# Sparse attention with MLP on one core: keys and values kept on row (token mod 128), values cast in place, SyncE and GpSimd in written order

## The chip, the cores and the metric

The kernel runs on one core of one Trainium2 chip. The metric is the device time of one execution in microseconds (us), on that core. Before the change the median of three runs is 268.42 us (268.03 to 269.17).

Engine names in the profile: PE is TensorE (PEld its weight loads), DVE is VectorE, ACT is ScalarE, POOL is GpSimd, SP is SyncE, SPq its DMA-issuing part.

## The reference

Sparse attention over 4 batches, 8 heads, 768 tokens and head size 64, followed by a two-layer MLP on the 3,072 tokens:

```python
k_sum = k.reshape(B, H, nb, 32, D).max(axis=3)      # one maximum key per block of 32
v_sum = v.reshape(B, H, nb, 32, D).mean(axis=3)     # one mean value per block
mask_l = np.abs(pos[:, None] - pos[None, :]) < 16   # local window
scores = concat([where(mask_l, q k^T * scale, -1e9), q k_sum^T * scale + log(32)])
x = softmax(scores) @ concat([v, v_sum])            # [B, H, S, D] -> [B*S, 512]
h = x @ w_in                                        # 512 -> 2048
out = (h * sigmoid(beta * h)) @ w_out               # 2048 -> 512
```

## The kernel before

Work is done in pairs of heads, four pairs to a batch, and in query tiles of 64. A query tile sees 96 window keys and 24 block keys, so 120 rows of a 128-row operand. The kernel builds these operands by copying: `kw` by VectorE from transposed keys, `vw` by 13 DMAs per batch. "(b, g)" below means pair g of batch b. Each batch has an **H stage** (16 h tiles, between them the keys and queries of the next batch) and an **O stage** (24 o parts, between them the attention of the next batch). Batch 0's attention has nothing to hide behind; it is **the head**.

```python
    # ... sizes: B=4, H=8, S=768, D=64; block=32, window=16, QT=64, KW=96, nb=24, VW=129; P=128
    q_r, k_r, v_r = (a.rearrange("b (g h) (c p e) d -> b g p (h c) (e d)", p=P, h=2, e=NE)
                     for a in (q, k, v))
    # ... 12 loads of batch 0 (k, q, v of four pairs) issued from SyncE and ScalarE; the later ones in stage()
    def load_pair(dst, src, b, g, nm):
        t = qk_pool.tile([P, nc3, NE, 2, D], bf16, name=nm, tag=nm)
        nc.gpsimd.tensor_copy(out=t[:], in_=stage(src, b, g, nm))
        dst[(b, g)] = t

    def load_v(b):
        for g in range(npair):
            nc.gpsimd.tensor_copy(
                out=vn_bufs[0][:, :, :, g, 0:2 * D].rearrange("p c e (h d) -> p c e h d", h=2),
                in_=stage(v_r, b, g, "v"))

    # ... constants on GpSimd: identity, bias, A_avg (block means as a matmul), band masks
    def scale_w_out(n):
        nc.vector.tensor_scalar(out=w_out_sb[:, n], in0=w_out_sb[:, n], scalar1=inv_beta[:, n:n + 1],
                                scalar2=None, op0=ALU.mult)
    def v_windows(b):
        vn, vw, vm = vn_bufs[0], vw_bufs[b % 2], vm_bufs[b % 2]
        vm_ps = ps.tile([P, npair, 2 * D], f32, name="vm_ps", tag="t", bufs=2)
        n = nc3 * NE
        for c in range(nc3):
            for e in range(NE):
                i = c * NE + e
                nc.tensor.matmul(vm_ps[:], A_avg[:, c, :], vn[:, c, e, :, 0:2 * D],
                                 start=(i == 0), stop=(i == n - 1))
        nc.vector.tensor_copy(out=vm[KW:P, :, 0:2 * D], in_=vm_ps[KW:P])
        vt = vw.rearrange("p (c u) g d -> p u c g d", u=P // QF)
        U = P // QF
        for e in range(NE):
            r0 = e * KF
            for u in range(U):
                lo, hi = u * QF - WF, u * QF - WF + KF
                a, z = max(lo, 0), min(hi, P)
                nc.sync.dma_start(out=vt[r0 + a - lo:r0 + z - lo, u], in_=vn[a:z, :, e])
                if lo < 0:
                    nc.sync.dma_start(out=vt[r0:r0 - lo, u, 1:], in_=vn[P + lo:P, 0:nc3 - 1, e])
                if hi > P:
                    nc.sync.dma_start(out=vt[r0 + P - lo:r0 + KF, u, 0:nc3 - 1], in_=vn[0:hi - P, 1:, e])
        nc.sync.dma_start(out=vw[KW:P], in_=vm[KW:P, None].to_broadcast([P - KW, nt, npair, VW]))

    def prep_pair(b, g):
        i = (b * npair + g) % NKW
        kw, q2 = kw_bufs[i], q2_bufs[i]
        kt, qt = ks.pop((b, g)), qs.pop((b, g))
        kwv = kw[:, :, 0:KW].rearrange("p t (e f) -> p t e f", e=NE)
        pk = ps.tile([P, NE, NF], bf16, name="pk", tag="t", bufs=2)
        for c in range(nc3):
            for e in range(NE):
                nc.tensor.transpose(pk[:, e, c * P:(c + 1) * P], kt[:, c, e], identity)
        inner = pk[:, :, QF - WF:QF - WF + KF]
        nc.vector.tensor_copy(out=kwv[:, 1:nt - 1],
                              in_=bass.AP(tensor=inner.tensor, offset=inner.offset,
                                          ap=[inner.ap[0], [QF, nt - 2], [NF, NE], [1, KF]]))
        nc.vector.tensor_copy(out=kwv[:, 0, :, WF:KF], in_=pk[:, :, 0:KF - WF])
        nc.vector.tensor_copy(out=kwv[:, nt - 1, :, 0:KF - WF], in_=pk[:, :, NF - KF + WF:NF])
        km = at_pool.tile([P, nb], bf16, name="km", tag="km")
        mid = kwv[:, :, :, WF:WF + QF]
        nc.vector.tensor_reduce(out=km.rearrange("p (t n) -> p t n", t=nt),
                                in_=bass.AP(tensor=mid.tensor, offset=mid.offset,
                                            ap=[mid.ap[0], mid.ap[1], [FB, QF // FB], mid.ap[2], [1, FB]]),
                                op=ALU.max, axis=mybir.AxisListType.XY)
        nc.vector.tensor_copy(out=kw[:, :, KW:KW + nb], in_=km[:, None].to_broadcast([P, nt, nb]))
        # ... the same for q: six transposes into pq, then copies into q2 on ScalarE and VectorE

    # ... scores(): s_ps = kw x q2, Exp on ScalarE into attn, mask on VectorE (batch 0: on TensorE)
    # ... av(): six matmuls a[:, t] x vw[:, t, g], reciprocal and two multiplies on VectorE into x_nat
    # ... x_transpose(): six transposes into px, copy into xT.  h_tile(): 8 matmuls + Silu.  o_part(): 4 matmuls
    for i in range(4):          # w_in, then w_out: issued from GpSimd, the scheduler decides when
        ...
    v_windows(0)
    prep_pair(0, 0)
    prep_pair(0, 1)
    all_scores(0, 0)
    prep_pair(0, 2)
    all_scores(0, 1)
    prep_pair(0, 3)
    all_scores(0, 2)
    load_beta()
    finish(0, 0)
    all_scores(0, 3)
    for g in range(1, npair):
        finish(0, g)
    # ... per batch: h_tile x 16, between them v_windows and the four prep_pair of the next batch;
    #     then (batch 0 only) the 16 scale_w_out; then o_part x 24, between them scores, av, x_transpose
```

A scheduler orders the instructions of every engine; the kernel's text fixes only what depends on what.

The softmax here doesn't subtract the row's maximum and nothing guards it: scores larger than these inputs give would overflow.

## Time and profile before

| | before |
|---|---|
| time, median of 3 | 268.42 us |
| span of the profiled run | 266.6 us |
| TensorE busy | 224.2 us (84%) |
| GpSimd busy | 49.3 us (18%) |
| DMA bytes | 35.83 MB |
| first h matmul of batch 0, which ends the head | 54.93 us |
| from there to the first h matmul of batch 1, then 2, then 3 | 53.27, 54.11, 54.12 us |
| rest (last batch) | 50.2 us |

The last three rows are read from TensorE's timeline: the start of the first `h_ps` matmul of each batch. They add up to the span, so a change of time can be put down to a stage.

The first lines to read are those of the page that cut the span in 40 slices of 6.7 us (busy tenths of TensorE, its granted clock in tenths, DMA busy tenths, and GB/s). Kernel before:

```profile
PE   0006924689999999999999999999999999999984
PEclk9999785979999999999999999999999999999999
DMA  7999999998799966119983111130011121000112
GB/s 194 268 290 288 221 239 223 231 267 167 169 295 291 207 174 218 42 39 239 291 176 101 50 66 46 39 59 2 0 42 39 39 81 39 0 2 37 61 62 78
```

TensorE works about a third of the first eight slices and is full from then on, while the DMA engines are full or nearly so up to the fourteenth. Two regimes, then: the head is bound by data and preparation, the rest by TensorE.

The table by stretches says how full. Columns after the stretch: its length, then busy us of PE, PEld, DVE, ACT, POOL (with instruction counts), granted clock, DMA share, GB/s. Kernel before, the second H stage and the second O stage:

```profile
core 0: us, PE busy (x) PEld busy (x) DVE busy (x) ACT busy (x) POOL busy (x), PEclk, DMA share, GB/s
108.20:136.55 28.35, 28.35 (x200) 17.33 (x198) 11.72 (x23) 17.07 (x20) 8.00 (x11) 1.00 0.67 169
136.55:162.31 25.76, 25.08 (x203) 14.32 (x201) 21.59 (x46) 10.66 (x12) 1.55 (x2) 1.00 0.26 75
```

TensorE is idle for 0 of 28.35 us in the H stage and 0.68 of 25.76 in the O stage. As long as TensorE's own work stays the same, no change of layout can take more than a microsecond from a batch here.

The chain of waits shows the head. Kernel before, start and length in us, then what the chain ran through:

```profile
2.47 13.10 DMA st_88<-in_v_dram
...
33.08 0.42 DVE kw_156 L240
33.50 10.36 DMA vw_163<-vm_161
...
43.95 1.46 PE av_ps L301 x12
```

It begins with 13.10 us of value loads. Later it waits 10.36 us for the window copies of the values. TensorE's own list of waits (what it waited for: us in total, times, longest) has the same two places. Kernel before:

```profile
PE vm_ps L208 <- POOL A_avg L131: 19.7, 1, 19.7
PE av_ps L301 <- DMA vw_163<-vm_161: 9.1, 1, 9.1
```

### The profile page before, as it was taken

The numbers are of one execution on the slowest core, as the hardware profiler recorded it, in microseconds if no ns is written. First come the engines' busy times: TensorE is split into PE (matmuls) and PEld (weight loads), VectorE is DVE, ScalarE is ACT, GpSimd is POOL, SyncE is SP. The second block draws the span as 40 slices with busy tenths as digits, with TensorE's granted clock in tenths as the row PEclk, the third lists the DMA queues.
The fourth block names the chain that finished last, engine by engine and source line by source line (L and its number), as shares of the span: only waits on it lengthen the run. The fifth ranks groups of instructions, "written<-read, shape, count | busy, mean of one in ns | idle before, by whom it ended". The sixth has DMA issues, their size and how long they took to land.

```text
span 266.6 us, 4089 instructions
## 1 busy us (share of the span) xinstructions
PE 224.2 (84%) x1609; PEld 132.2 (50%) x1609; DVE 138.4 (52%) x302; ACT 112.7 (42%) x128; POOL 49.3 (18%) x80
## 2 busy tenths in 40 slices
PE   0006924689999999999999999999999999999984
PEld 0003713545665555456665554566656545664431
DVE  7106532796687888314678884245788751001221
ACT  0102760447778231077783330567842405672000
POOL 3169704151245200024420000020000000000000
PEclk9999785979999999999999999999999999999999
DMA  7999999998799966119983111130011121000112
GB/s 194 268 290 288 221 239 223 231 267 167 169 295 291 207 174 218 42 39 239 291 176 101 50 66 46 39 59 2 0 42 39 39 81 39 0 2 37 61 62 78
DMA packets 51986, 35.83 MB, mean 134 GB/s; under 512 B 1904, under 2 KB 48896, under 8 KB 51968
## 3 DMA queue, kind: packets, MB, share of 16 engines
q1 hardware_dynamic: 43040, 29.03, 41.4%
q0 software_dynamic: 4224, 4.19, 9.4%
q10 hardware_dynamic: 4704, 2.36, 3.4%
q8 instruction: 12, 0.20, 0.3%
q14 instruction: 6, 0.05, 0.1%
HBM read 27.27 MB, written 6.29 MB: 126 GB/s over the span
## 4 chain that ended last, share of the span: by engine, by line
PE 63%; DVE 15%; DMA 9%; ACT 4%; POOL 4%; issue 3%; SPq 1%; POOLq 0%; ACTq 0%
PE h_ps L332 32%; PE o_ps L345 19%; DVE x_nat L306 7%; DMA st_88<-in_v_dram 5%; DMA vw_163<-vm_161 4%; ACT attn L284 3%; PE s_ps L281 3%; DVE attn L287 3%; PE px L317 2%; PE av_ps L301 2%; DVE o_sb L349 2%; PE pk L238 2%; PE vm_ps L208 1%; PE pq L255 1%; DVE r L303 1%
## 5 line engine op out<-in xcount | busy, mean ns | idle before, releaser
L345 PE MATMUL o_ps<-w_out_sb,h_sb 128*128 128x512 bf16 x384 | 92.7, 379 | 0.9 <-DVE o_sb L349 0.8
L332 PE MATMUL h_ps<-xT,w_in_sb 128*128 128x384 bf16 x512 | 88.3, 329 | 0.0
L334 ACT ACTIVATE h_sb<-h_ps,beta_sb 128x768 bf16<-128x768 f32 x64 | 57.2, 900 | 45.8 <-PE h_ps L332 45.7
L332 PEld LDWEIGHTS <-w_in_sb 128*128 128x128 bf16 x512 | 49.9, 99 | 33.4 <-issue 1.0
L345 PEld LDWEIGHTS <-h_sb 128*128 128x128 bf16 x384 | 35.7, 98 | 34.8 <-issue 1.6
L284 ACT ACTIVATE attn<-s_ps,bias 128x768 bf16<-128x768 f32 x32 | 28.0, 899 | 40.2 <-PE s_ps L281 32.3
L349 DVE COPY o_sb<-o_ps 128x512 f32<-128x512 f32 x24 | 16.5, 689 | 48.9 <-PE o_ps L345 48.6
L306 DVE TENSOR_TENSOR x_nat<-av_ps,r 64x384 bf16<-64x384 f32 x64 | 35.5, 555 | 1.5
L208 PE MATMUL vm_ps<-vn_82,A_avg 128*128 128x512 bf16 x24 | 7.5, 443 | 19.7 <-POOL A_avg L131 19.7
L301 PEld LDWEIGHTS <-attn 128*128 128x128 bf16 x192 | 13.7, 101 | 16.9 <-issue 10.7
L94 POOL CAST k_nat<-st 128x768 bf16<-128x768 f32 x12 | 10.2, 854 | 61.7 <-issue 41.8
L105 POOL CAST vn_82<-st 128x768 bf16<-128x768 f32 x12 | 9.7, 834 | 48.7 <-PE vm_ps L208 29.8
L287 DVE TENSOR_TENSOR attn<-attn,band 128x768 bf16<-128x768 bf16 x24 | 13.9, 581 | 6.9 <-ACT attn L284 6.5
L301 PE MATMUL av_ps<-vw_163,attn 128*128 128x129 bf16 x96 | 8.5, 232 | 10.2 <-DMA vw_163<-vm_161 9.1
L208 PEld LDWEIGHTS <-A_avg 128*128 128x128 bf16 x24 | 2.5, 108 | 22.5 <-POOL A_avg L131 20.0
L317 PE MATMUL px<-identity,x_nat 128*128 128x128 bf16 x96 | 8.7, 231 | 4.2 <-DVE x_nat L306 3.9
L303 DVE RECIPROCAL r<-av_ps 128x6 f32<-128x6 f32 x32 | 6.1, 193 | 11.0 <-PE av_ps L301 10.5
L317 PEld LDWEIGHTS <-x_nat 128*128 128x128 bf16 x96 | 5.8, 102 | 11.3 <-DVE x_nat L306 11.3
L94 POOL CAST q_nat<-st 128x768 bf16<-128x768 f32 x12 | 10.1, 840 | 6.9 <-DMA st<-in_q_dram 6.5
L210 DVE CAST vm_161<-vm_ps 32x512 bf16<-32x512 f32 x2 | 1.4, 700 | 19.1 <-PE vm_ps L208 19.1
L334 ACT ACT_TABLE_LOAD x4 | 5.1, 1283 | 11.6 <-PE h_ps L332 11.6
L255 PE MATMUL pq<-identity,q_nat 128*128 128x128 bf16 x96 | 8.2, 223 | 2.2 <-DVE kw_154 L244 2.1
(118 smaller groups left out, 188.7 us busy)
## 6 DMA issues: line engine op xcount, KB each, us to landing
out_dram<-o_sb SPq DMA_DIRECT2D x24, 256.0 KB
st<-in_v_dram SPq DMA_DIRECT2D x12, 384.0 KB
st<-in_k_dram SPq DMA_DIRECT2D x12, 384.0 KB
st<-in_q_dram SPq DMA_DIRECT2D x12, 384.0 KB
w_in_sb<-in_moe_w_in_dram POOLq DMA_DIRECT2D x4, 512.0 KB, 10.4
w_out_sb<-in_moe_w_out_dram POOLq DMA_DIRECT2D x4, 512.0 KB, 20.4
vw_163<-vn_82 SPq DMA_DIRECT2D x8, 145.1 KB
vw_164<-vn_82 SPq DMA_DIRECT2D x8, 145.1 KB
```

What stands on the lines that cost most here:

```text
L94: nc.gpsimd.tensor_copy(out=t[:], in_=stage(src, b, g, nm))
L208: nc.tensor.matmul(vm_ps[:], A_avg[:, c, :], vn[:, c, e, :, 0:2 * D], start=(i == 0), stop=(i == n - 1))
L255: nc.tensor.transpose(pq[:, e, c * P:(c + 1) * P], qt[:, c, e], identity)
L284: nc.scalar.activation(out=sl.rearrange("p (k j) h q -> p k (j h q)", k=2), in_=big[:, :, 0:w], func=ACTF.Exp, bias=bias[:], scale=scale)
L287: nc.vector.tensor_mul(out=sl, in0=sl, in1=band[:, None, None, :].to_broadcast([P, 2 * TB, 2, QT]))
L301: nc.tensor.matmul(ov[:, m // AB, m % AB], a[:, t], vw[:, t, g, :], start=True, stop=True)
L306: last["norm"] = nc.vector.tensor_mul(out=x[par * QT:(par + 1) * QT, :, hh, :].rearrange("p (k j) d -> p k j d", k=2), in0=ov[lo:lo + D, : ...
L317: nc.tensor.transpose(px[:, c * P:(c + 1) * P], x[:, c], identity)
L332: nc.tensor.matmul(big[:, kk, 0:MG], w_in_sb[:, ki, ni * P:(ni + 1) * P], xT[b][:, ki, kk * MG:(kk + 1) * MG], start=(ki == 0), stop=(ki = ...
L334: nc.scalar.activation(out=h_bufs[(b, ni // 8)][:, ni % 8, :].rearrange("p (k m) -> p k m", k=2), in_=big[:, :, 0:MG], func=ACTF.Silu, sca ...
L345: nc.tensor.matmul(o_ps, h_bufs[(b, ni // 8)][:, ni % 8, ms * P:(ms + 1) * P], w_out_sb[:, ni, :], start=(ni == 0), stop=(ni == k2 - 1))
L349: nc.vector.tensor_copy(out=o_sb[:], in_=o_ps)
```

## The change

The intent is to stop copying windows. A 128-token tile of keys or values stays where its token number puts it, on row (token mod 128). For the even 64-query half of a tile, the 16 rows at the far end hold the neighbour's edge and the 24 block rows overwrite rows that this half does not see; the odd half is the mirror image. So each tile needs two variants (`ve`, `vo`; `kw[:, 0]`, `kw[:, 1]`). A value tile is cast twice, directly into both, and four small DMAs per pair add edges and block means; 13 window DMAs per batch go. Values are now prepared per pair, behind the keys, not all at the start. The loads of v have rows of 256 bytes where they had 512. One line more keeps SyncE's and GpSimd's instructions in the order in which the text has them.

```diff
+    ctx.enter_context(tc.manual_schedule(engines={mybir.EngineType.SP, mybir.EngineType.Pool}))
 ...
-    q_r, k_r, v_r = (a.rearrange("b (g h) (c p e) d -> b g p (h c) (e d)", p=P, h=2, e=NE)
-                     for a in (q, k, v))
+    q_r, k_r = (a.rearrange("b (g h) (c p e) d -> b g p (h c) (e d)", p=P, h=2, e=NE) for a in (q, k))
+    v_r = v.rearrange("b (g h) (c p) d -> b g p (h c) d", p=P, h=2)
 ... (staging per pair, masks for both halves, larger memsets on VectorE)
-    def v_windows(b):
 ... (13 DMAs into vw)
+    def prep_v(b, g):
+        ve, vo = ve_bufs[b % 2][g], vo_bufs[b % 2][g]
+        f = staged.pop(("v", b, g)).rearrange("p (h c d) -> p c h d", h=2, d=D)
+        nc.gpsimd.tensor_copy(out=ve[:, 0:nch, 0:2 * D]..., in_=f)
+        nc.gpsimd.tensor_copy(out=vo[:, 1:, 0:2 * D]..., in_=f)
+        vm_ps = ps.tile([P, 2 * D], f32, name="vm_ps", tag="t", bufs=2)
+        for c in range(nch):
+            nc.tensor.matmul(vm_ps[:], A_avg[:, c, :], ve[:, c, 0:2 * D], ...)
+        vm = x_pool.tile([nb, 2 * D], bf16, name="vm", tag="vm")
+        nc.scalar.copy(out=vm[:], in_=vm_ps[0:nb])
+        nc.sync.dma_start(out=vo[0:W, 1:], in_=ve[0:W, 1:])
+        nc.sync.dma_start(out=ve[P - W:P, 0:nch], in_=vo[P - W:P, 0:nch])
+        src = vm[:, None].to_broadcast([nb, nch, 2 * D])
+        nc.sync.dma_start(out=ve[SUM[0]:SUM[0] + nb, 0:nch, 0:2 * D], in_=src)
+        nc.sync.dma_start(out=vo[SUM[1]:SUM[1] + nb, 1:, 0:2 * D], in_=src)
 ...
-    def prep_pair(b, g):
+    def prep_qk(b, g):
+        kt, qt = cast_qk("k", b, g), cast_qk("q", b, g)      # two casts on GpSimd
 ... (transposes into pk as before)
+        cv(out=kwv[:, 0, :, 0:hi], in_=pkv[:, :, 0:hi])                       # VectorE
+        cv(out=kwv[:, 0, 1:, F - w:F], in_=pkv[:, 0:nch - 1, F - w:F])
+        ca(out=kwv[:, 1, :, lo:F], in_=pkv[:, :, lo:F])                       # ScalarE in batch 0
+        ca(out=kwv[:, 1, 0:nch - 1, 0:w], in_=pkv[:, 1:, 0:w])
         nc.vector.tensor_reduce(out=km[:], ...)
-        nc.vector.tensor_copy(out=kw[:, :, KW:KW + nb], in_=km[:, None].to_broadcast([P, nt, nb]))
+        for par in range(2):
+            nc.gpsimd.tensor_copy(out=kw[:, par, :, SUM[par]:SUM[par] + nb],
+                                  in_=km[:, None].to_broadcast([P, nch, nb]))
 ...
+    prep_qk(0, 0); load3(0, 2); prep_v(0, 0); prep_qk(0, 1); both_scores(0, 0); load3(0, 3)
+    prep_v(0, 1); prep_qk(0, 2); both_scores(0, 1); prep_v(0, 2); load_w_in(0); finish(0, 0)
+    prep_qk(0, 3); both_scores(0, 2); prep_v(0, 3)
+    for i in range(1, 4):
+        load_w_in(i)
 ... (rest of batch 0, then load3(1, 0), load3(1, 1))
 ... (between h tiles: prep_qk and prep_v of each pair of the next batch, load3 two pairs ahead)
+                    if b == 0 and g == 1:            # after prep_qk(1, 1)
+                        for i in range(4):
+                            load_w_out(i)
```

(The calls of batch 0 stand one to a line in the kernel.)

## The prediction

> **What bounds the kernel now.** Two regimes. From 57.7 us on, TensorE is the limit: the table by stretches shows it busy 27.0 of 27.0 us (55-82), 28.0 of 28.0 (108.5-136.5) and 25.3 of 26.0 (136.5-162.5), clock 1.00; the chain of waits is h_ps and o_ps matmuls. One batch takes 54.1 us; layout can shorten that by 1 us at most. Before 57.7 us (the last first-batch px transpose) lies the head: TensorE first works at 19.7 us, and the chain there is the v loads (13.1 us), GpSimd casts and constants (15.6 to 27.7), then 10.4 us waiting for the vw window copies queued behind other transfers (33.5 to 43.9).
>
> **What the change does.** Removed: 13 window DMAs per batch (1.6 MB), and the wait for all four v tiles. Added: a second v cast per pair (0.83 us GpSimd), two km copies per pair on GpSimd (estimate 0.45), four small DMAs per pair, 256-byte v rows in the loads (the Trainium skill, "DMA: Bandwidth & Descriptors", Specifications, puts line rate at 512 B and more; this trace has no 256-byte load, so estimate +0.5 us a tile). VectorE per later pair: kw copies become interleaved (0.96 us per 768 elements for q2 today), about +0.4 us, in H stages where VectorE has room. Memsets of whole tiles (about 13 us in all) now precede the first kw copy on VectorE.
>
> **Head, estimated by walking the queues.** GpSimd is in order ("PSUM — Partial Sum Buffer", Engine vs sequencer instructions: strict FIFO), so a pair costs a loop: k,q casts 1.7; q copies and kw copies on ScalarE/VectorE 2.7; reduce 0.95; km 0.45; v casts 1.7; about 7.6 us. First km about 17 us (memsets), fourth about 40.5; then v casts, small DMAs, av, norms, px: last px about 50.7 instead of 57.7. Gain about 7 us.
>
> **Where it is given back.** Weights now queue behind the casts on GpSimd: w_in quarters 2-4 issue about 43, w_out only after the km copies of pair (1,1), about 11 us into the first H stage (62), landing about 77 behind w_in and the batch-1 loads (about 10 us per weight, estimated from the saturated 22-50 us stretch). VectorE's queue puts 15 of 16 w_out scalings ahead of pair (1,2)'s kw copies; TensorE's queue puts vm of pair (1,2) after two o_ps matmuls. H work ends near 73; TensorE then waits to about 83 (scale 1.5, kw+reduce 2.4, km 0.45, ve cast 0.83). The second half of preparation moves into the first O stage, where VectorE is already 84% busy: +1 to 2 us. Later batches: 0 to +1 each. Net: -7 + about 10 (less 1, plus 1.4 for moved transposes) + 1 + 1 = a few us either way.
>
> **Prediction.** 270.5 us, range 259 to 281. Faster by over 2%: 0.27; within 2%: 0.42; slower by over 2%: 0.31. I pull the sum (about +4) down, since the stall rests on contended transfers.
>
> **What would show it.** Head: last first-batch px transpose near 51; GpSimd idle between its q casts and km copies, waiting on VectorE reduces, about 4 us per pair; no 10 us wait on a vw-type DMA. Give-back: one long TensorE wait between 72 and 86, vm_ps or o_ps, ended by a GpSimd ve cast, with VectorE waiting on the w_out DMA just before; w_out landing near 77. Steady batches: 54 to 55 us as before. DMA bytes down 4 MB; GpSimd busy up 15 us.
>
> **What would make it wrong.** w_out landing before about 68: then no stall, and about 262. The head loop shorter (ScalarE copies faster, memsets cheaper): about 258. Above 280: 256-byte loads at twice the time, or SyncE's order starving each H stage.

## The result, and the profile after

The changed kernel takes 287.09 us (median of 4 runs, 286.74 to 288.30), the kernel before 268.51 us beside it (268.03 to 269.17). The ratio is 1.0698 with a 95% interval of 1.0659 to 1.0737, so it is 7% slower, and outside the predicted range of 259 to 281. Ratios here are the mean time of one kernel's runs over that of the other's of the same rounds, so not quite the ratio of the medians that are quoted.

| us | before | after | difference |
|---|---|---|---|
| span of the profiled run | 266.6 | 285.0 | +18.4 |
| start of the first h matmul | 54.93 | 53.24 | -1.7 |
| from there to the next batch's h | 53.27 | 67.69 | +14.4 |
| second batch | 54.11 | 56.95 | +2.8 |
| third batch | 54.12 | 56.69 | +2.6 |
| rest | 50.2 | 50.4 | +0.3 |
| GpSimd busy | 49.3 | 69.2 | +19.9 |
| DMA bytes, MB | 35.83 | 31.63 | -4.2 |

The 40 slices of the kernel after (7.1 us each):

```profile
PE   1266650999907599999899999998999999999984
PEclk9997785699975989999999999999999999999999
DMA  7937239969990079120780890108801102000111
GB/s 186 268 57 184 34 62 182 253 152 223 196 230 18 8 205 249 39 75 12 179 189 16 217 235 37 74 14 183 190 18 56 60 37 74 2 0 2 74 74 75
```

Two things stand out against the lines of before. TensorE starts sooner, but its row has two zeros, in the seventh slice (43 to 50 us, in the head) and in the twelfth (78 to 86 us, **the hole** below), with the clock row down to 0.5 in or just after each. And the DMA engines, which moved 194 to 290 GB/s all through the old head, now move 57, 34 and 62 GB/s in three slices of the first six. The weights that used to travel then have not been asked for yet.

The table by stretches of the kernel after. The columns are those of the table of before. The first lines are the hole and the 13 us after it, the last two the second H and O stages, for comparison with the lines of before:

```profile
78.00:87.00 9.00, 0.59 (x3) 0.19 (x2) 5.65 (x14) 0.69 (x2) 1.25 (x3) 0.70 0.93 191
87.00:100.00 13.00, 9.13 (x69) 6.07 (x71) 8.75 (x16) 6.81 (x10) 4.88 (x8) 0.76 0.07 16
...
120.93:150.82 29.89, 28.42 (x212) 17.78 (x211) 14.40 (x29) 17.86 (x26) 11.15 (x18) 1.00 0.45 110
150.82:177.88 27.06, 25.78 (x204) 14.80 (x206) 20.64 (x42) 11.08 (x14) 3.75 (x6) 1.00 0.52 132
```

In the second H stage TensorE now idles 1.47 us (0 before), in the O stage 1.28 us (0.68 before). TensorE's work has hardly grown (28.42 against 28.35 us, 25.78 against 25.08).

TensorE's two longest waits in the kernel after:

```profile
PE vm_ps L183 <- POOL ve_152 L179: 8.5, 1, 8.5
...
PE av_ps L265 <- DMA ve_149<-vm: 7.4, 1, 7.4
```

The 9.1 us wait for window copies is gone, as intended. In its place stand one wait for a value cast on GpSimd (the hole) and one for a small DMA of block means (in the head).

**The loop in the head.** GpSimd's timeline of the kernel after (start, length, instruction, and in brackets the idle time before it and what ended that):

```profile
24.68 0.83 POOL L173 CAST k_nat<-hold_84 128x768 bf16<-128x768 f32 x1
25.46 0.83 POOL L173 CAST q_nat<-hold_85 128x768 bf16<-128x768 f32 x1
30.25 0.56 POOL L218 COPY kw_140<-km 128x144 bf16<-128x144 bf16 x2 [3.97 <-DVE km L215]
30.76 0.83 POOL L179 CAST ve_148<-hold_86 128x768 bf16<-128x768 f32 x1
...
32.30 0.89 POOL L332 DMA_DIRECT2D w_in_sb<-in_moe_w_in_dram  x1
33.18 0.84 POOL L173 CAST k_nat<-hold_84 128x768 bf16<-128x768 f32 x1
```

GpSimd casts k and q of a pair, then sits 3.97 us until VectorE has reduced that pair's keys, because the copies of the reduced keys (L218) stand next in its order. Only after them come the value casts and the next pair's k. A round takes 7.3 to 9.0 us (the copies are at 15.36, 22.64, 30.25 and 39.29 us); GpSimd has 3.9 us of casts and copies in it. The Trainium skill, "PSUM — Partial Sum Buffer", section Engine vs sequencer instructions, calls the queues of ScalarE, VectorE and GpSimdE strict FIFO; the trace agrees, nothing passes the waiting copy.

**The end of the head.** GpSimd's and SyncE's DMA issues, and the matmul group that waits (kernel after):

```profile
41.33 2.23 POOL L332 DMA_DIRECT2D w_in_sb<-in_moe_w_in_dram  x3
...
42.77 0.87 SPq L189 DMA_DIRECT2D ve_149<-vm  x1
...
49.83 0.81 PE L265 MATMUL av_ps<-ve_149,attn 128*128 128x129 bf16 x6 [7.39 <-DMA ve_149<-vm]
```

Three quarters of `w_in` are issued at 41.33 us, the block means of the last pair just behind them. These are 36 KB (24 rows of 6 times 256 bytes), yet TensorE waits 7.39 us for the first of them.

**The hole.** TensorE, VectorE and GpSimd around 78 to 87 us (kernel after):

```profile
66.79 2.97 POOL L335 DMA_DIRECT2D w_out_sb<-in_moe_w_out_dram  x4
...
82.41 0.88 DVE L165 TENSOR_SCALAR w_out_sb<-w_out_sb,inv_beta 128x512 bf16<-128x512 bf16 x3 [2.25 <-DMA w_out_sb<-in_moe_w_out_dram]
83.30 0.66 DVE L210 COPY kw_140<-pk 128x480 bf16<-128x480 bf16 x1
...
84.74 0.95 DVE L215 TENSOR_REDUCE km<-pk 128x24 bf16<-128x768 bf16 x1
...
85.75 0.56 POOL L218 COPY kw_140<-km 128x144 bf16<-128x144 bf16 x2 [12.87 <-DVE km L215]
86.25 0.83 POOL L179 CAST ve_152<-st 128x768 bf16<-128x768 f32 x1
...
87.13 0.80 PE L183 MATMUL vm_ps<-ve_152,A_avg 128*128 128x128 bf16 x6 [8.55 <-POOL ve_152 L179]
```

Read it from the bottom up. TensorE waits for a value cast; GpSimd makes that cast after a copy for which it idled 12.87 us; the copy needs a reduction on VectorE; VectorE's key copies stand behind a scaling of `w_out`; the scaling waits for `w_out`; and `w_out` was issued at 66.79 us only, in GpSimd's order behind the same kind of copy of the pair before. One late weight, three in-order queues, and TensorE busy for 0.59 of 9 us.

### The profile page after: what moved, and what is told of

Same layout as the page of the kernel before. It is cut to its first block, busy times and chain, and to the rows that moved or that the text cites. A ratio compares the mean times of both kernels' runs of the same rounds, so it can differ in the third digit from the quotient of the medians.

```text
span 285.0 us, 4358 instructions
## 1 busy us (share of the span) xinstructions
PE 231.5 (81%) x1664; PEld 140.0 (49%) x1681; DVE 142.8 (50%) x331; ACT 121.4 (43%) x172; POOL 69.2 (24%) x122
## 2 busy tenths in 40 slices
DMA packets 63669, 31.63 MB, mean 111 GB/s; under 512 B 31376, under 2 KB 60576, under 8 KB 63648
## 4 chain that ended last, share of the span: by engine, by line
PE 46%; DVE 18%; issue 11%; POOL 8%; ACT 7%; DMA 6%; SPq 2%; POOLq 0%; ACTq 0%
PE o_ps L309 21%; PE h_ps L296 15%; ACT attn L250 4%; DVE x_nat L270 3%; DMA st<-in_q_dram 3%; DVE km L215 3%; PE px L281 3%; DMA vo_157<-vm 3%; DVE attn L253 2%; PE s_ps L248 2%; PE av_ps L265 2%; PE vm_ps L183 2%; PE pk L203 1%; DVE o_sb L313 1%; POOL q_nat L173 1%
## 5 line engine op out<-in xcount | busy, mean ns | idle before, releaser
L296 PEld LDWEIGHTS <-w_in_sb 128*128 128x128 bf16 x512 | 49.2, 98 | 30.7 <-issue 1.0
L309 PEld LDWEIGHTS <-h_sb 128*128 128x128 bf16 x384 | 36.5, 99 | 38.7 <-issue 6.2
L265 PEld LDWEIGHTS <-attn 128*128 128x128 bf16 x192 | 14.5, 105 | 15.8 <-issue 9.1
L253 DVE TENSOR_TENSOR attn<-attn,band 128x768 bf16<-128x768 bf16 x24 | 15.0, 627 | 8.6 <-ACT attn L250 8.2
L215 DVE TENSOR_REDUCE km<-pk 128x24 bf16<-128x768 bf16 x16 | 15.2, 950 | 2.9 <-ACT kw_139 L213 1.7
L183 PEld LDWEIGHTS <-A_avg 128*128 128x128 bf16 x96 | 8.1, 111 | 15.6 <-DVE km L215 7.6
L218 POOL COPY kw_138<-km 128x144 bf16<-128x144 bf16 x8 | 2.2, 308 | 52.8 <-DVE km L215 52.8
L203 PE MATMUL pk<-identity,k_nat 128*128 128x128 bf16 x96 | 9.3, 242 | 6.4 <-POOL k_nat L173 6.4
L203 PEld LDWEIGHTS <-k_nat 128*128 128x128 bf16 x96 | 7.5, 109 | 9.1 <-POOL k_nat L173 6.6
L165 DVE TENSOR_SCALAR w_out_sb<-w_out_sb,inv_beta 128x512 bf16<-128x512 bf16 x16 | 5.2, 386 | 10.4 <-DMA w_out_sb<-in_moe_w_out_dram 10.3
L298 ACT ACT_TABLE_LOAD x4 | 5.1, 1283 | 11.4 <-PE h_ps L296 11.3
```

The source lines that it names most:

```text
L215: nc.vector.tensor_reduce(out=km[:], in_=pk.rearrange("p e (n f) -> p n e f", f=block // NE), op=ALU.max, axis=mybir.AxisListType.XY)
L253: nc.vector.tensor_mul(out=a, in0=a, in1=band[:, par, None, None, :].to_broadcast([P, nch, 2, QT]))
L265: nc.tensor.matmul(ov[:, m // TB, m % TB], a[:, m], vt[:, m], start=True, stop=True)
L296: nc.tensor.matmul(big[:, kk, 0:MG], w_in_sb[:, ki, ni * P:(ni + 1) * P], xT[b][:, ki, kk * MG:(kk + 1) * MG], start=(ki == 0), stop=(ki = ...
L298: nc.scalar.activation(out=h_bufs[(b, ni // 8)][:, ni % 8, :].rearrange("p (k m) -> p k m", k=2), in_=big[:, :, 0:MG], func=ACTF.Silu, sca ...
L309: nc.tensor.matmul(o_ps, h_bufs[(b, ni // 8)][:, ni % 8, ms * P:(ms + 1) * P], w_out_sb[:, ni, :], start=(ni == 0), stop=(ni == k2 - 1))
```

## The experiments

The theory after this reading: the time went to the written order of GpSimd, (a) because it issues the weights late, (b) because value casts stand behind copies that wait for VectorE. Rivals: the layout itself (256-byte rows, more copies, VectorE load); written order as such, whatever the layout; and transfers, which no reordering mends. All ratios are against the kernel before, in the same rounds. The table at the end of this section has all stages.

### Weights earlier in GpSimd's order

`e1_wout_head`: `w_out` directly behind `w_in`.

```diff
     for i in range(1, 4):
         load_w_in(i)
+    for i in range(4):
+        load_w_out(i)
 ...
-                    if b == 0 and g == 1:
-                        for i in range(4):
-                            load_w_out(i)
```

> The changed kernel, with only the four w_out loads moved in GpSimd's written order: from behind the mask copies of pair (1,1) to right behind the w_in loads, about 25 us earlier. Theory (weights queue too late behind casts): the 8.5 us wait of TensorE for the v cast of pair (1,2) goes, and with it the low clock behind it; time 287 to about 274-277 (w_out now shares the transfer engines with the first batch-1 loads, so a few us come back in the first H stage). Rival (the loss lies in the layout: 256-byte loads, more casts, more copies): 284-288.

Measured: 282.81 us, ratio 1.0522 [1.049, 1.0555], missed the expected 274 to 277. The hole at the o matmuls is gone, but batch 1 takes 63.33 us (67.69 after). Now the first H stage is long, 53.78 to 90.65. TensorE's waits in it, and the `w_out` issues (KB each, median us from issue to landing):

```profile
PE pq L223 <- POOL q_nat L173: 6.5, 3, 5.2
```

```profile
w_out_sb<-in_moe_w_out_dram POOLq DMA_DIRECT2D x4, 512.0 KB, 18.9
```

In the kernel after, `w_out` took 9.8 us. Here it shares the transfers with `w_in` and batch 1's loads, and TensorE waits for q casts whose loads come late. So moving `w_out` gains 4 us, and the rest looks like a debt of bytes: what was not moved while the DMA engines stood at 34 and 62 GB/s has to be moved later, beside something that is needed then. The theory in its simple form (the weights are late, so issue them earlier) is only partly right.

`e2_gap`: all the weights as early as the gaps in the loop allow.

```diff
+        if b == 0 and g in (1, 2):          # in prep_qk, right after the k and q casts
+            for n in range(4):
+                (load_w_in if g == 1 else load_w_out)(n)
 ... (the other issues of weights removed)
```

> The changed kernel, with all w_in issues placed between the casts and the mask copies of pair (0,1), and all w_out issues likewise in pair (0,2), where GpSimd waits 3.6 and 4 us for the reduce anyway. Theory: the stall before the first o stage goes as in e1, and the 7.4 us wait for the block-mean DMA of pair (0,3), which ran beside three w_in transfers, shrinks to about 3; head ends near 51 instead of 55.4; time about 268-271. Rival (layout costs it): not below 280. If the 7.4 us wait was not the weights but the DMA's own length, e2 equals e1 within 1 us.

Measured: 288.60 us, ratio 1.0738 [1.0705, 1.0771]; 268 to 271 was expected, a clear miss. Batch 1 falls to 56.69 us, so the hole is gone. But the head grows to 65.68 us. TensorE's wait there, and SyncE's issue of a small copy:

```profile
PE av_ps L268 <- DMA ve<-vm: 19.6, 2, 17.5
```

```profile
25.93 10.24 SPq L186 DMA_DIRECT2D vo<-ve  x1
```

The issue alone held SyncE for 10.24 us (the same kind of issue took 0.59 us at 41.41 us of the kernel after), and TensorE waited 17.5 us for block means; 11.56 us of them are the DMA of the block means itself. The new layout puts on its critical path, once per pair, what the old one had once per batch: small DMAs that queue behind large ones. The Trainium skill, "DMA: Bandwidth & Descriptors", section Issuing engines are not separate DMA queues, says that DMAs of SyncE and GpSimd run on the same 16 engines and interleave. This run agrees: weights issued from GpSimd delay copies issued from SyncE.

### Layout or order: the two-by-two

`e3_after_scheduled` drops the new line from the kernel after; `e4_before_written` adds it to the kernel before.

```diff
-    ctx.enter_context(tc.manual_schedule(engines={mybir.EngineType.SP, mybir.EngineType.Pool}))
```

> The changed kernel without its line that keeps SyncE and GpSimd in written order: new layout, scheduler's order. Theory (most of the loss is in the written order, not the layout): clearly below the changed kernel, 266-278. Rival (layout): 284-290. The scheduler puts all first-batch casts and w_in ahead of the first mask copy, so the head may be longer than in the changed kernel while the stall at the first o stage is shorter.

> The kernel before, with the line added: old layout, written order. Its text issues all weights before the second batch's casts, so theory (what hurts is where the weights stand in the order, not keeping the order as such) expects 266-276. Rival (keeping the written order is itself costly): 280 and more.

Measured:

| | scheduled | SyncE and GpSimd in written order |
|---|---|---|
| old layout | 268.8 (the kernel before, same chip) | 276.61, ratio 1.0285 [1.0257, 1.0314] |
| new layout | 277.06, ratio 1.0307 [1.0276, 1.0338] | 287.09, ratio 1.0698 |

The line costs 8 us in the old layout and 10 in the new, the layout 8 us scheduled and 10 ordered. (The bottom-right run is of another chip call.) But equal totals hide different places. With the new layout and a free scheduler the steady batches take 54.38 and 54.25 us (54.11 and 54.12 before): so the layout, with its 256-byte rows, its copies and its small DMAs, costs **0.3 us at most** in a steady batch. Of its 8 us, 6.3 lie in the head (61.18 us), where the scheduler puts other casts and `w_in` ahead of the first copies on GpSimd, and 2.1 in batch 1. TensorE's wait in that head:

```profile
PE s_ps L247 <- POOL kw L217: 17.1, 2, 9.7
```

The old layout in written order (just above its expected range) has its time in other places than the kernel before. TensorE's first h matmul, and its longest wait after it:

```profile
43.56 2.27 PE L333 MATMUL h_ps<-xT,w_in_sb 128*128 128x384 bf16 x6
...
56.47 1.01 PE L209 MATMUL vm_ps<-vn,A_avg 128*128 128x512 bf16 x2 [9.15 <-POOL vn L106]
```

The head ends 11.4 us earlier than before, with the old layout and its window copies. The scheduler had SyncE issue batch 1's value loads first (from 14.79 us) and the window copies behind them (22.23 to 34.1 us). In written order the copies are issued from 14.06 to 26.0 us and the loads after them, and TensorE's 9.1 us wait for window copies is gone. So the long wait that the change set out to remove came from what stood ahead of the copies and beside them (the value loads, and the weights, issued from 23.3 us on before and from 25.5 us here), and one line removed it; the run does not separate the two. The gain does not last. Those value loads are now issued beside the weights, TensorE waits 9.15 us for a value cast, and batch 1 takes 64.41 us: its end comes at 107.97 us, as before (108.20). The 8 us are lost in the later batches (58.53 and 58.34 us). In the text their value loads stand behind output stores (issued at 114.01 us, after six stores), and TensorE waits there twice for value casts, 3.0 us in all, a part only of the 4 us per batch. So written order as such is not free for a text that was not written for it; the rival is partly right.

### The loop: casts before copies, or copies elsewhere

`e5_v_first` moves only the two value casts ahead of the copies that wait.

```diff
+    def cast_v(b, g):        # the two value casts of prep_v, called in prep_qk right after the k and q casts
```

> The changed kernel with each pair's two v casts written before its mask-row (km) copies instead of after, so they run while GpSimd waits for VectorE's reduce. Theory (GpSimd's written order makes one loop per pair: casts, wait for the reduce, km copies, v casts): 1.7 us leave the loop; steady batches 56.9 to 54.5-55.5 us, first h matmul at 53.2 to about 49-51, the stall before the first o stage stays; time 287 to 277-281. Rival (steady batches are longer because the new layout has more copies and matmuls, 24 instead of 6 for vm): steady batches stay at 56.5-57.

Measured: 271.54 us, ratio 1.0088 [1.0032, 1.0145]; 15.5 us less than after, about twice what was expected. (The profiled run is its fastest, 268.79.) The head ends 10 us earlier, at 43.20, and the later batches take 55.49 and 54.28 us. The kernel after had 56.95 and 56.69. In batch 1 (63.67 us) a wait of the old kind is left: VectorE's key copies stand behind the scaling of the late `w_out` there too.

```profile
PE vm_ps L186 <- DVE km L219: 7.2, 1, 7.2
```

`e6_km_vector` leaves the casts and moves the copies to the engine that makes their input.

```diff
-            nc.gpsimd.tensor_copy(out=kw[:, par, :, SUM[par]:SUM[par] + nb],
+            nc.vector.tensor_copy(out=kw[:, par, :, SUM[par]:SUM[par] + nb],
```

> The changed kernel with the km copies on VectorE, where the kernel before had them, so GpSimd never waits for VectorE. Theory: the loop is broken, steady batches 54.3-55 us, w_out is issued some 10 us earlier (GpSimd only waits for loads), TensorE's 8.5 us wait for the v cast falls below 4; but the block-mean DMA still runs beside w_in; time 268-276. Rival (transfer capacity, not GpSimd order, sets when w_out lands): stall unchanged, above 279.

Measured: 264.94 us, ratio 0.9884 [0.9835, 0.9932]: 22 us less than after by one word, and below the expected range. GpSimd's timeline in the head and at the weights:

```profile
9.19 0.83 POOL L173 CAST q_nat<-hold 128x768 bf16<-128x768 f32 x1 [3.23 <-DMA hold<-in_q_dram]
9.96 0.83 POOL L179 CAST ve<-hold 128x768 bf16<-128x768 f32 x1
...
11.51 0.83 POOL L173 CAST k_nat<-hold 128x768 bf16<-128x768 f32 x1
...
47.06 2.97 POOL L335 DMA_DIRECT2D w_out_sb<-in_moe_w_out_dram  x4
...
63.51 0.83 POOL L173 CAST k_nat<-st 128x768 bf16<-128x768 f32 x1 [11.88 <-DMA st<-in_k_dram]
```

The casts now run back to back. `w_out` is issued at 47.06 us (66.79 after), although its place in the text is the same: the order now waits for nothing but loads. The hole is gone and the head ends at 40.17 us. What is left is in batch 1 (62.33 us): pair (1, 2) comes late (63.51), again because loads stand behind weights.

### 256-byte rows

`e7_v_rows_512B` loads the values with the old 512-byte rows into the new layout; its **result is wrong** (relative error 0.259), since rows land on other tokens.

```diff
-    v_r = v.rearrange("b (g h) (c p) d -> b g p (h c) d", p=P, h=2)
+    v_r = v.rearrange("b (g h) (c p e) d -> b g p (h c) (e d)", p=P, h=2, e=NE)
```

> Wrong result on purpose: the changed kernel, but v loaded with the 512-byte pattern of k and q (each partition gets two neighbouring tokens); everything behind the loads is unchanged. Theory: the 256-byte rows cost at most a few us, where transfers are saturated (w_out landing, batch-1 loads): 283-287. Rival (256-byte rows take about twice the time, 16 v tiles, and this is the main loss): below 280.

Measured: 286.55 us, ratio 1.0671 [1.0635, 1.0707]; the kernel after is at 1.0698, so the difference is half a microsecond, within the intervals. The line of the DMA queue (packets, MB, time of its packets as a share of 16 engines), first of the kernel after, then of this one:

```profile
q1 hardware_dynamic: 56304, 25.97, 36.5%
```

```profile
q1 hardware_dynamic: 44784, 25.97, 32.8%
```

The same bytes in 11,520 fewer packets take 3.7% of 285 us less, 10.5 us over the 15 value tiles of this queue, so 0.7 us a tile. The Trainium skill, "DMA: Bandwidth & Descriptors", section Specifications, asks for 512 bytes or more for line rate; the runs agree in direction, and show the cost to be almost wholly off the critical path here.

### `w_in`, `w_out` and the wait behind each

`e9_w_in_gap3` issues the last three quarters of `w_in` one gap earlier.

```diff
+        if (b, g) == (0, 3):                # in prep_qk, right after the k and q casts
+            for n in range(1, 4):
+                load_w_in(n)
```

> The changed kernel, with only the w_in issues 2 to 4 moved ahead, from behind the v casts of pair (0,3) to behind its k and q casts (GpSimd idles there 4.5 us for the reduce): about 6.5 us earlier, into a stretch where transfers are nearly idle. Theory: TensorE's 7.4 us wait for the block-mean DMA of pair (0,3) is the w_in traffic beside it, and falls to about 3; first h matmul 53.2 to about 49; the stall later stays; 283-284. Rival (that DMA is slow by itself, or waits for its semaphores): wait stays at 7, time 287.

Measured: 284.93 us, ratio 1.0619 [1.0592, 1.0646], a microsecond above the expected range. TensorE's waits in the whole stretch of 40 to 100 us:

```profile
PE vm_ps L183 <- POOL ve L179: 11.3, 2, 10.1
PE av_ps L268 <- DMA ve<-vm: 2.9, 1, 2.9
```

The wait for block means falls from 7.4 to 2.9 us and the head ends 2.9 us earlier. So `w_in` in transfer was what the small DMA waited for. But the hole grows from 8.5 to 10.1 us, and about 2 us of the gain arrive at the end (287.09 to 284.93).

`e10_no_w_out_scaling` leaves out the scaling of `w_out`, so that VectorE's queue does not wait for it (**wrong**, relative error 0.689).

```diff
-        if b == 0:
-            with tc.issue_after(last["norm0"].ins):
-                for n in range(k2):
-                    scale_w_out(n)
```

> Wrong result on purpose: the changed kernel without the 16 VectorE multiplications that scale w_out, so o matmuls wait for the w_out transfer itself and nothing on VectorE does. Theory (VectorE's queue, blocked on the late w_out, holds back the kw copies of pair (1,2), hence km, v cast, vm on TensorE): the 8.5 us wait for the v cast goes, TensorE works on o tiles as the quarters land (until about 82) and the second h stage starts 4-8 us earlier; 279-283. Rival (w_out landing late is all that matters, the queue order nothing): second h stage within 2 us of 120.9 less the 5 us of saved VectorE time off the path, 285-287.

Measured: 278.72 us, ratio 1.0397 [1.0356, 1.0438], 0.3 us below the expected range. The profiled run is the slowest of the four, 281.18. In it the wait for the value cast, 8.5 us before, has gone from the stretch of 60 to 100 us:

```profile
PE vm_ps L183 <- POOL ve L179: 0.2, 1, 0.2
```

`w_out` is as late as ever, in GpSimd's order at the same place, and yet no wait there is longer than 3.6 us (for a key cast). The late weight hurt through VectorE's queue: its scalings stood ahead of key copies that had nothing to do with them. (The edit also takes 5.2 us of work off VectorE, so the gain in time need not all come from the order; that the wait goes is read from the trace.)

### Together

`e8_combined` has both edits of `e5` and `e6`, the loads of pairs (0, 2) and (0, 3) before everything, `w_in` behind the casts of pair (0, 1) and `w_out` behind those of pair (1, 0).

```diff
+    load3(0, 2); load3(0, 3)          # ahead of prep_qk(0, 0)
 ... (edits of e5 and e6; w_in after the casts of (0, 1), w_out after the casts of (1, 0))
```

> All together: km copies on VectorE, v casts with the k and q casts, all first-batch loads issued up front, w_in issued behind the casts of pair (0,1), w_out behind the casts of pair (1,0). Theory: transfers no longer idle in the head, weights land before they are needed, no loop: first h matmul at 45-50, steady batches 54.3-55, no wait over 3 us at the first o stage; 258-266, faster than both. Rival (the small DMAs of the new layout wait behind whatever large transfers are in flight, as in e2): head above 55 and time 270 or more.

Measured: 270.74 us, ratio 1.0093 [1.0046, 1.014]. This missed 258 to 266 and is worse than `e6` alone. TensorE's wait in the head:

```profile
PE av_ps L275 <- DMA ve<-vm: 9.5, 2, 8.4
```

Once more the block means behind the weights. Nor does batch 1 gain by the early weights (62.94 us against 62.33 in `e6`): TensorE still waits 5.9 us there for a key reduction, which stands behind the scaling of `w_out` on VectorE.

`e11_best` has the edits of `e5` and `e6` only, and issues the loads of the pair after next right behind a pair's casts.

```diff
+        cast_v(b, g)                        # in prep_qk, right after the k and q casts
+        if b > 0 and g + 2 < npair:
+            load3(b, g + 2)
 ... (load3 removed from behind prep_v; copies of km on VectorE)
```

> e6 (km copies on VectorE) with the v casts next to the k and q casts, and the loads of pair g+2 of later batches issued right behind the casts that free their buffers, ahead of that pair's small DMAs. In e6 TensorE waited 5.8 us in the first h stage for the k load of pair (1,2), issued at 52 behind the small DMAs and beside w_out. Theory: it is issued near 45, that wait goes: 258-262, faster than the kernel before by 2.5-4% . Rival (transfers are saturated there, the wait only moves to another load or to w_out): 263-266.

Measured: 262.57 us (median of 6), ratio 0.9779 [0.9744, 0.9814], a correct result: 2.2% faster than the kernel before, though the interval reaches over the 2% line, so "unclear" by that measure. The median misses the expected 262 by half a microsecond. The head ends at 39.81 us, and the steady batches take 54.75 and 54.24. The longest wait left in batch 1 is 3.7 us, again for a key reduction behind the scaling of `w_out`.

### All stages

| us | first h | batch 1 | batch 2 | batch 3 | rest | time |
|---|---|---|---|---|---|---|
| before | 54.93 | 53.27 | 54.11 | 54.12 | 50.2 | 268.5 |
| after | 53.24 | 67.69 | 56.95 | 56.69 | 50.4 | 287.1 |
| `e1_wout_head` | 53.78 | 63.33 | 56.71 | 57.08 | 50.4 | 282.8 |
| `e2_gap` | 65.68 | 56.69 | 57.12 | 56.86 | 50.5 | 288.6 |
| `e3_after_scheduled` | 61.18 | 55.37 | 54.38 | 54.25 | 50.4 | 277.1 |
| `e4_before_written` | 43.56 | 64.41 | 58.53 | 58.34 | 50.3 | 276.6 |
| `e5_v_first` | 43.20 | 63.67 | 55.49 | 54.28 | 50.5 | 271.5 |
| `e6_km_vector` | 40.17 | 62.33 | 54.94 | 55.16 | 50.5 | 264.9 |
| `e7_v_rows_512B` (wrong result) | 53.10 | 67.93 | 56.57 | 56.70 | 50.5 | 286.6 |
| `e8_combined` | 45.54 | 62.94 | 55.06 | 55.30 | 50.5 | 270.7 |
| `e9_w_in_gap3` | 50.35 | 69.54 | 57.02 | 56.94 | 50.5 | 284.9 |
| `e10_no_w_out_scaling` (wrong result) | 53.94 | 60.99 | 56.94 | 57.13 | 50.5 | 278.7 |
| `e11_best` | 39.81 | 61.41 | 54.75 | 54.24 | 50.5 | 262.6 |

(Stages are of the profiled run, times are medians.) Read down the columns: in the new layout, the kernels with value casts behind the waiting copies on an ordered GpSimd have steady batches near 57 us, and the others 54 to 55.5. The runs with the loop broken have a head of 40 to 46 us, and batch 1 near 61 to 64 us is where all of them pay part of it back. `e4_before_written`, which never had the loop, shows the same pair of numbers in the old layout.

## Why the prediction was wrong

The prediction saw the mechanism and mis-sized its terms, nearly all to one side. Its sum as written is -7 + 10 - 1 + 1.4 + 1 + 1 = +5.4 us (the text says "about +4"), against +18.4 measured:

| term | predicted | measured | error |
|---|---|---|---|
| head | -7 | -1.7 | +5.3 |
| batch 1 (hole, moved transposes, O stage) | +11.4 | +14.4 | +3.0 |
| later batches, together | +1 | +5.4 | +4.4 |
| rest | 0 | +0.3 | +0.3 |

**Right.** The loop: predicted 7.6 us a round, with the fourth copy at 40.5; measured 7.3 to 9.0, fourth at 39.29. The hole: predicted as `w_out` issued at 62, landing at 77, TensorE waiting until 83 for a GpSimd cast behind VectorE's scalings; measured 66.79, 82.4 and 87.1, the same chain link by link, and `e10_no_w_out_scaling` takes it away. The length (8.5 us against "about 10") was fine as well, though both ends came 4 to 6 us later than predicted (78.6 and 87.1 us against 73 and 83). DMA bytes -4.2 MB (-4 predicted). GpSimd busy +19.9 us (+15 predicted, somewhat short). The 256-byte rows: 0.7 us a tile against the estimate of 0.5, which no trace stood behind; off the critical path.

**Wrong: "then v casts, small DMAs, av, norms, px: last px about 50.7 instead of 57.7. Gain about 7 us".** The last px of batch 0 ended at 55.40 us, against 57.72 before: 2.3 us gained (1.7 by the first h matmul, which the table has). The step that failed is the landing of the block means: it was taken as prompt, and was 7.39 us late behind `w_in`, which the prediction itself had put at "about 43", next to them. It costed the traffic for `w_out` and not for the small copy. `e9_w_in_gap3` shows it: with `w_in` earlier the wait falls to 2.9 us and the last px ends at 52.5, so that what is left of the wait covers the rest of the error.

**Wrong: "Later batches: 0 to +1 each".** Measured +2.8 and +2.6. The text saw the loop of casts, copies and value casts in the head only; it also runs in every later H stage, where a round takes 6.7 to 7.4 us and TensorE has 6.2 us of work to cover it. TensorE's waits for casts add up to 1.8 and 1.7 us in these two batches of the kernel after (none before); a part of the rest is TensorE's own busy time (54.20 and 53.97 us against 53.43 and 53.44). `e5_v_first` (55.5, 54.3) and `e6_km_vector` (54.9, 55.2) break the loop, these waits fall to 0.5 and 0.9 us over both batches together, and the batches return for the most part; `e3_after_scheduled` (54.4, 54.3) keeps the layout and drops the order, with the same effect. So it is the written order of value casts after the waiting copies, and not the layout.

**Wrong in size: "The second half of preparation moves into the first O stage ... +1 to 2 us".** The O stage took 33.8 us (87.1 to 120.9) against 26.7 (81.5 to 108.2), +7.1. Three contributions can be seen in the trace from 87 to 100 us. TensorE does the block means of pairs (1, 2) and (1, 3) and the transposes of (1, 3) there, 2.7 us. It waits another 1.2 us for a value cast and 2.1 us for VectorE's output copy. And o matmuls take 494 ns in the mean instead of 379 (15 of them, 1.7 us), at a mean granted clock of 0.76. The Trainium skill, "TensorE: Matmul & The Clock Gate", Part 1: The HAM clock gate, says that the clock follows how busy the array was of late, at half rate after an idle window of about 3.4 us. The trace agrees for the hole: the clock is 0.50 from 81.5 us, 2.9 us after the last matmul, to 91.7 us, 4.6 us after the restart, and 1.00 in steady batches. It is 0.50 once more from 98.6 to 102.0 us, from the second of the two short waits on. The prediction priced the wait and left out the slow restart. No run isolates these three from each other.

**And the pull.** The sum was shaded from +4 to +2.1 "since the stall rests on contended transfers". The contention lay on the other side: the block means, taken as prompt, came 7.39 us late. The transfer of `w_out` itself was predicted well (15.6 us from issue to the last landing, 15 predicted); it ended late because GpSimd's order issued it 4.8 us later than assumed.

What stays open: batch 1 takes 61 to 64 us in all the kernels with the short head, the old layout in written order included, 8 to 11 us over before. The longest waits there are for a load (a key in `e6`, 5.8 us; a value in `e4`, 9.15 us) or, in `e5`, `e8` and `e11` (7.2, 5.9 and 3.7 us), for a key reduction behind the scaling of `w_out` on VectorE: the queue of the hole once more. No run takes the scaling out of these kernels, and none separates how much of the rest is bytes put off from the head and how much is order.

## What to carry to other kernels

On an engine that runs its instructions in written order, each instruction that waits for another engine holds up all that follows, the DMA issues as well. So place such an instruction on the engine that produces its input, or behind everything that does not need it: one word did that here, worth 22 us. When a change makes small DMAs part of the critical path, look up which large transfers are issued just ahead of them; issuing the weights earlier moved the wait more often than it removed it. Before a layout is changed to be rid of a wait for a DMA, look at what stands ahead of that DMA and beside it: `e4_before_written` lost the 9.1 us wait without a new layout. And look at the DMA row of the slices before looking at any wait: transfers that a head does not make have to be made later, though no run here isolates what that costs.

## What the Trainium skill lacked or had wrong

- "DMA: Bandwidth & Descriptors" says that queues interleave packet by packet on shared engines, and gives no figure for what a small DMA waits beside large ones. Here DMAs of 36 KB, issued next to transfers of 512 KB, held TensorE for 7.4 us (after), 17.5 us (`e2_gap`, 11.6 of them in the DMA itself) and 8.4 us (`e8_combined`); with the weights out of the way it was 2.9 us (`e9_w_in_gap3`).
- The same page says that initiating a DMA takes the sequencer's time and that it is usually small; it has no figure for an issue that is held back. One issue on SyncE took 10.24 us in `e2_gap`, against 0.59 us in the kernel after.
- The same page, Specifications: rows under 512 bytes miss line rate. The page has an overhead per packet for descriptors of 256 bytes, but no time for a tile or a kernel: here 256-byte rows took 0.7 us more of queue time for a tile of 384 KB, and at most about half a microsecond of the whole run, which is within the intervals.
- "TensorE: Matmul & The Clock Gate" ties the half clock to an idle window of about 3.4 us and does not say how busy a window must be to count as busy. In the kernel after, the clock fell to 0.50 at 98.6 us although TensorE had been busy for 1.27 of the 3.4 us before; no wait there was longer than 2.1 us.
